# The second MLP layer of the last batch as seven block products (Strassen) on one Trainium2 core

## The chip, the cores and the metric

One core of one Trainium2 chip runs the whole program. The metric is the time of one execution on the device in microseconds (us). A change counts as faster or slower when the 95% interval of the ratio is clear of 2%, as the same when the interval lies within 2%, else as unclear.

In the profiles, PE is TensorE (matmuls), PEld its weight loads, DVE VectorE, ACT ScalarE, POOL GpSimd, SP the engine that issues transfers. L173 and the like are lines of the program; one helper at L173 issues nearly all matmuls, so one tells groups apart by the tiles that they write and read.

## The reference, cut to what matters

```python
# block-sparse attention of 4 batches, 8 heads, 768 positions, 64 per head -> x: (4, 768, 512)
scores = scale * q @ k^T;  scores = where(mask, scores, -1e9);  attn = softmax(scores)
x = (attn @ v) with the heads side by side
# mixer on x
h = (x^T @ U @ V)^T            # U: 768x32, V: 32x768
u = x + h
out = u + relu(u @ w_ch1) @ w_ch2      # w_ch1: 512x2048, w_ch2: 2048x512
```

The change concerns the last product, `relu(...) @ w_ch2`, for the last of the four batches: 768 x 2048 times 2048 x 512.

## The kernel before: the parts that matter

The Python program places every instruction in a fixed order per engine. A small model of time (`clk`) decides, while the program is built, what is put next on TensorE: score units, value products and MLP steps of the batch before are interleaved, so that TensorE always has work. On the chip that order is fixed.

Attention for one head pair has nine units. A unit is: score matmuls into a two-bank PSUM tile (`double`), an exponential on ScalarE into an SBUF tile `est`, then a product with the mask on VectorE, with both inputs in SBUF:

```python
def mask_mul(u, est):
    ...
    nc.vector.tensor_tensor(out=o, in0=o, in1=m, op=ALU.mult)     # 128 x 1024, f16
    return 1.25 if clk["pool"] > clk["dve"] else 0.69             # us, for the model
```

After nine units come the values (`pav`, 72 matmuls), a normalization on VectorE (`rcp`, `xs`), a cast on GpSimd (`xh`), the low-rank product (`pa`), its sum on VectorE (`a`), the second one (`ph`), and the addition `xf` on VectorE. GpSimd also issues the loads of q, k and v:

```python
def unit_sides(i, u):            # called when unit u of head pair i is put in order
    ...
    if u in (3, 5, 7):
        load_cast(i + 2, {3: "q", 5: "k", 7: "v"}[u])             # GpSimd issues two transfers
```

PSUM has eight banks, used as four tiles of two banks each, handed out by `double(name)` and given back by `give_back`. The second layer of the last batch used one bank of such a tile per 128 rows (a row group):

```python
def w2(sc, part, n0, n1):
    if part == 0:
        pair["pch"] = double("pch")                  # tile [128, 2, 512] f32
    pch = pair["pch"][:, 0:1, 0 : n1 - n0]
    for jj in range(4 * part, 4 * part + 4):         # 16 in all
        mm(pch[:, 0, :], tT[jj][:, sc * P : (sc + 1) * P], w2t[:, jj, n0:n1], jj == 0, jj == NJJ - 1)
    if part == 3:
        leave(sc, 1, n0, n1, pch, pair["pch"])       # one VectorE addition, one transfer out
```

The softmax here doesn't subtract the row's maximum and nothing guards it: scores larger than these inputs give would overflow.

## Time and profile before

| | before |
|---|---|
| time, median of 4 runs (lowest, highest) | 278.81 us (277.80, 279.37) |
| span of the profiled execution | 276.6 us |
| first layer of the last batch, 128 matmuls | 232.09 to 252.90 us |
| second layer of the last batch | 252.90 to 273.82 us: 20.92 us |
| last matmul's end to the end of the span | 2.8 us |

The lines behind these numbers are in the prediction below.

One view: the mask products as a group, with busy time, mean ns of one, and idle time before them. In the kernel before:

```profile
L520 DVE TENSOR_TENSOR est<-est,m 128x1024 f16<-128x1024 f16 x108 | 78.3, 740 | 18.2 <-ACT est L499 16.8
```

### The profile page before, as it was taken

Reading aid. Unit: us, or ns where it says so; the run is one execution under the profiler, and the core shown is the slowest. Engines: PE = TensorE matmul, PEld = TensorE weight load, DVE = VectorE, ACT = ScalarE, POOL = GpSimd, SP = SyncE. Lnnn points to the kernel's source line nnn. Section 1 sums busy time; section 2 is a strip of 40 time slices with the busy share of each in tenths; the row PEclk is TensorE's granted clock in tenths of the full one; section 3 lists DMA queues with packets and bytes.
Section 4 is the critical chain, followed back from the end, with each engine's and each line's share of the span. In section 5 each row is a group of like instructions: output and inputs, shape, how many; then the busy total and the mean of one; then the engine's idle time right before and its main releaser. Section 6 shows DMA issues by size and latency. Waiting matters only on the chain.

```text
span 276.6 us, 8037 instructions
## 1 busy us (share of the span) xinstructions
PE 270.9 (98%) x3493; PEld 161.8 (59%) x3493; DVE 175.2 (63%) x286; ACT 177.3 (64%) x198; POOL 103.2 (37%) x137
## 2 busy tenths in 40 slices
PE   8999999999999999999999999999999999999995
PEld 2577775565656564656565565656565654665443
DVE  6877758878797987777756768777777451000112
ACT  3999995877897857694955749584886201664000
POOL 5659639407274835363604536361102020000000
PEclk9999999999999999999999999999999999999999
DMA  6999976999979999996990989995100322000222
GB/s 202 287 297 258 264 172 104 165 185 87 142 47 107 174 125 145 157 105 73 59 112 0 189 88 164 135 100 74 31 2 2 104 79 79 27 1 0 78 77 76
DMA packets 85484, 31.65 MB, mean 114 GB/s; under 512 B 75152, under 2 KB 83048, under 8 KB 85448
## 3 DMA queue, kind: packets, MB, share of 16 engines
q0 software_dynamic: 49824, 10.29, 43.8%
q1 hardware_dynamic: 35268, 20.62, 34.7%
q8 instruction: 27, 0.44, 0.7%
q10 hardware_dynamic: 356, 0.22, 0.3%
q14 instruction: 9, 0.07, 0.1%
HBM read 27.84 MB, written 6.29 MB: 123 GB/s over the span
## 4 chain that ended last, share of the span: by engine, by line
PE 83%; ACT 11%; DVE 2%; DMA 1%; issue 1%; POOL 1%; SPq 0%; DVEq 0%; POOLq 0%; ACTq 0%
PE pch L173 30%; PE pt L173 30%; ACT est L499 11%; PE pav L173 11%; PE psc L173 9%; PE pa L173 2%; DMA qld<-in_q_dram 1%; PE ph L173 1%; POOL xh L599 0%; DVE xh L542 0%; DVE xs L590 0%; PE pmk L173 0%; POOL qst L247 0%; PE pturn L266 0%; PE puT L704 0%
## 5 line engine op out<-in xcount | busy, mean ns | idle before, releaser
L499 ACT ACTIVATE est<-psc 128x1024 f16<-128x1024 f32 x144 | 143.2, 1028 | 45.4 <-PE psc L173 43.7
L173 PE MATMUL pt<-uT,w1t 64*128 64x384 f16 (+1 forms) x896 | 94.4, 324 | 0.0
L173 PE MATMUL pch<-w2t,tT 64*128 64x512 f16 (+3 forms) x688 | 93.6, 372 | 0.1
L520 DVE TENSOR_TENSOR est<-est,m 128x1024 f16<-128x1024 f16 x108 | 78.3, 740 | 18.2 <-ACT est L499 16.8
L173 PEld LDWEIGHTS <-w1t 64*128 64x128 f16 (+1 forms) x896 | 46.0, 95 | 36.1 <-PE pt L173 8.3
L173 PEld LDWEIGHTS <-tT 64*128 64x128 f16 (+1 forms) x688 | 38.2, 95 | 36.9 <-PE pch L173 1.6
L737 ACT ACTIVATE tT<-pt 128x768 f16<-128x768 f32 (+1 forms) x48 | 36.6, 772 | 26.0 <-PE pt L173 26.0
L173 PEld LDWEIGHTS <-est 128*128 128x128 f16 x1152 | 41.5, 97 | 10.9 <-issue 5.0
L173 PE MATMUL pav<-vt,est 128*128 128x65 f16 x1152 | 44.5, 193 | 0.1
L792 DVE TENSOR_TENSOR of<-xf,pch 128x1024 f32<-128x1024 f32 (+3 forms) x16 | 15.2, 950 | 42.7 <-PE pch L173 42.7
L173 PE MATMUL psc<-qT,kT 64*128 64x512 f16 (+1 forms) x288 | 40.6, 323 | 0.3 <-ACT est L499 0.3
L599 POOL CAST xh<-xs 128x768 f16<-128x768 f32 x12 | 10.5, 872 | 79.1 <-DVE xs L590 73.5
L685 POOL CAST uh<-xf 128x768 f16<-128x768 f32 x12 | 14.0, 1163 | 26.1 <-DVE xf L676 14.5
L173 PE MATMUL psc<-qa,ka 128*128 128x512 f16 (+1 forms) x96 | 21.7, 326 | 0.4 <-ACT est L499 0.2
L739 DVE TENSOR_SCALAR tT<-pt 128x768 f16<-128x768 f32 (+1 forms) x20 | 18.3, 917 | 5.9 <-PE pt L173 5.8
L173 PEld LDWEIGHTS <-kT 64*128 64x128 f16 x288 | 14.6, 94 | 12.5 <-issue 0.7
L261 POOL DMA_DIRECT2D vt<-in_v_dram x20 | 16.3, 821 | 3.8 <-DMA w2t<-in_moe_w_ch_dram 3.8
L261 POOL DMA_DIRECT2D qst<-in_q_dram x20 | 16.3, 820 | 0.1
L261 POOL DMA_DIRECT2D kst<-in_k_dram x20 | 16.3, 819 | 0.0
L590 DVE TENSOR_TENSOR xs<-pav,rcp 128x768 f32<-128x768 f32 x12 | 11.5, 958 | 1.2
L676 DVE TENSOR_TENSOR xf<-xs,ph 128x768 f32<-128x768 f32 x12 | 11.4, 950 | 1.2 <-PE ph L173 1.2
L173 PEld LDWEIGHTS <-ka 128*128 128x128 f16 (+1 forms) x108 | 8.7, 97 | 3.9 <-issue 2.0
(70 smaller groups left out, 131.2 us busy)
## 6 DMA issues: line engine op xcount, KB each, us to landing
out_dram<-of SPq DMA_DIRECT2D x9, 512.0 KB, 3.3
vld<-in_v_dram SPq DMA_DIRECT2D x6, 384.0 KB, 8.0
w1t<-in_moe_w_ch_dram POOLq DMA_DIRECT2D x4, 512.0 KB, 9.2
w2t<-in_moe_w_ch_dram POOLq DMA_DIRECT2D x4, 512.0 KB, 11.0
qld<-in_q_dram SPq DMA_DIRECT2D x5, 384.0 KB, 7.2
kld<-in_k_dram SPq DMA_DIRECT2D x5, 384.0 KB, 8.3
qst<-in_q_dram POOLq DMA_DIRECT2D x20, 96.0 KB, 4.1
kst<-in_k_dram POOLq DMA_DIRECT2D x20, 96.0 KB, 4.6
```

What stands on the lines that cost most here:

```text
L173: ins = nc.tensor.matmul(out, lhsT, rhs, start=start, stop=stop, skip_group_check=loose)
L261: keep(nc.gpsimd.dma_start(out=o[:, h], in_=src_of(nm, i)[:, h]))
L499: keep(nc.scalar.activation(out=est, in_=psc, func=AF.Exp, scale=0.125))
L520: keep(nc.vector.tensor_tensor(out=o, in0=o, in1=m, op=ALU.mult))
L590: nc.vector.tensor_tensor(out=xs.rearrange("p (c j) (h d) -> p c (j h) d", c=2, h=2), in0=pv[:, :, :, 0:D], in1=rcp[:, :, :, None].broadca ...
L599: keep(nc.gpsimd.tensor_copy(out=xh, in_=xs))
L676: nc.vector.tensor_tensor(out=u.rearrange("p (c j) n -> p c j n", c=2), in0=xs.rearrange("p (c j) n -> p c j n", c=2), in1=ph[:, :, 0:HS]. ...
L685: keep(nc.gpsimd.tensor_copy(out=uh, in_=u))
L737: keep(nc.scalar.activation(out=o, in_=i, func=AF.Relu))
L739: keep(nc.vector.tensor_scalar_max(out=o, in0=i, scalar1=0.0))
L792: nc.vector.tensor_add(out=of, in0=xfs[b][:, sc : sc + nsc, n0:n1], in1=pch)
```

## The change

The intent: a product of two 2x2 block matrices needs seven block products in place of eight, so TensorE streams an eighth less in that layer. The price is sums of blocks. Five sums of weight blocks go to GpSimd, in ten instructions amid attention; the sums of activation blocks go to VectorE during the first layer, where it is idle; and the outputs are put together by VectorE, in place in `xf`. Cut to its core:

```diff
+    W_SUMS = {"11+22": ..., "12-22": ..., "21-11": ..., "11+12": ..., "21+22": ...}
+    def add_w2(n):                                  # n = 0..9
+        ...                                         # even n: 6 of 8 blocks (1536), odd n: 2 of 8 (512)
+        keep(nc.gpsimd.tensor_tensor(out=o, in0=w2_block(x0, y0, j0, j1),
+                                     in1=w2_block(x1, y1, j0, j1), op=op))
...
+        def add_t(j):                               # activations, VectorE, after two relus
+            for o, i0, i1, op in (
+                (both, lo, hi, ALU.add),                               # 768 elements
+                (diag, lo[:, 0:HS], hi[:, HS:S], ALU.add),             # 384
+                (lo[:, HS:S], lo[:, HS:S], lo[:, 0:HS], ALU.subtract),
+                (hi[:, 0:HS], hi[:, 0:HS], hi[:, HS:S], ALU.subtract),
+            ): keep(nc.vector.tensor_tensor(out=o, in0=i0, in1=i1, op=op))
...
-        for jj in range(NJJ):                       # order of the first layer's blocks
+        for jj in range(NJJ) if rowed else [j + x * NJ for j in range(NJ) for x in range(2)]:
...
-        def w2(sc, part, n0, n1): ...
+        def w2_product(g, n, j0, j1, n0=0, n1=HB):  # g: pair of row groups, n: product
+            if n == 3 and j0 == 0: pair["ab", g] = double("pab")       # both banks in one tile
+            if n == 1 and j0 == 0: pair["c", g] = double("pc")
+            bank, at = {3: (0, 0), 5: (0, HB), 4: (1, 0), 2: (1, HB), 1: (2, 0),
+                        6: (0, 0), 7: (1, 0)}[n]
+            o = c[:, 0, 0:HB] if bank == 2 else ab[:, bank, at : at + HB]
+            for j in range(j0, j1): mm(o, t_sum[n, j][:, g * P : (g + 1) * P], w[:, n0:n1], ...)
+            def run(eng):                           # VectorE, when the model has time for it
+                if n == 5: acc(c11, ab[:, 0, HB:512], ALU.subtract); acc(c12, ab[:, 0, HB:512])
+                           acc(c12, ab[:, 0, 0:HB]); send(c12)
+                if n == 2: ...                      # three or four sums out of ab[:, 1]
+                if n == 1: ...                      # c11 and c22 from c
+                if n == 6: acc(c22, ab[:, 0, 0:HB]); send(c22)
+                if n == 7: acc(c11, ...); send(c11, n0, n1)
...
+        for g in range(3):
+            for n in (3, 5, 4, 2, 1, 6, 7): ...     # the last of all in two pieces of columns
...
     def unit_sides(i, u):
+        if u in (1, 6) and i in range(2 * HP, 3 * HP + 1):
+            add_w2(2 * (i - 2 * HP) + (u == 6))
```

More of the change, by code (lines that the diff above doesn't have):

```diff
@@ L714, in turn_u_pe, with w2_block @@
         run_on("dve", 0.6)
+    NJ, HB = NJJ // 2, HD // 2
+    W_SUMS = {
+        "11+22": (0, 0, 1, 1, ALU.add),
+        "12-22": (0, 1, 1, 1, ALU.subtract),
+        "21-11": (1, 0, 0, 0, ALU.subtract),
+        "11+12": (0, 0, 0, 1, ALU.add),
+        "21+22": (1, 0, 1, 1, ALU.add),
+    }
+    w_sum = {}
+    def w2_block(x, y, j0, j1):
+        return w2t[:, x * NJ + j0 : x * NJ + j1, y * HB : (y + 1) * HB]
+    def add_w2(n):
+        k, part = n // 2, n % 2
+        key = list(W_SUMS)[k]
+        x0, y0, x1, y1, op = W_SUMS[key]
+        if n == 0:
+            for m in range(6):
+                t = ldpool.tile([P, 6, HB], FP16, tag="ld" + "qkv"[m % 3], name="w2s")
+                w_sum["home", m] = t
+        j0, j1 = ((0, 6), (6, NJ))[part]
+        if part == 0:
+            o = w_sum["home", k][:, 0:6, :]
+        elif k < 3:
+            o = w_sum["home", 5][:, 2 * k : 2 * k + 2, :]
+        else:
+            o = qa[0][k - 3].rearrange("p (j n) -> p j n", n=HB)[:, 0:2, :]
+        keep(
+            nc.gpsimd.tensor_tensor(
+                out=o, in0=w2_block(x0, y0, j0, j1), in1=w2_block(x1, y1, j0, j1), op=op
+            )
+        )
+        for j in range(j0, j1):
+            w_sum[key, j] = o[:, j - j0, :]
     def mlp_steps(b):
@@ L741, in run @@
                 give_back(pt, clk[eng] + us)
+                if not rowed:
+                    jj = tiles[0][0]
+                    full.add(jj)
+                    if (jj + NJ) % NJJ in full:
+                        later("dve", 1, lambda e: add_t(jj % NJ), clk[eng] + us)
                 return us
@@ L749, in tile_of @@
             return tT[jj]
+        rowed = b < B - 1
+        full, t_sum, added = set(), {}, set()
+        def add_t(j):
+            lo, hi = tT[j], tT[NJ + j]
+            if j % 2 == 0:
+                t_sum["two"] = new_est().rearrange("p a n -> p (a n)")
+            both = new_est().rearrange("p a n -> p (a n)")[:, 0:S]
+            diag = t_sum["two"][:, (j % 2) * HS : (j % 2 + 1) * HS]
+            for o, i0, i1, op in (
[3 more added lines that the diff above has]
+                (hi[:, 0:HS], hi[:, 0:HS], hi[:, HS:S], ALU.subtract),
+            ):
+                keep(nc.vector.tensor_tensor(out=o, in0=i0, in1=i1, op=op))
+            t_sum[1, j] = diag
+            t_sum[2, j] = both[:, HS:S]
+            t_sum[3, j] = lo[:, 0:HS]
+            t_sum[4, j] = hi[:, HS:S]
+            t_sum[5, j] = both[:, 0:HS]
+            t_sum[6, j] = lo[:, HS:S]
+            t_sum[7, j] = hi[:, 0:HS]
+            added.add(j)
+            return 1.5
@@ new lines, in force, with acc, send @@
+        def force(done):
+            while not done():
+                clk["pe"] += 0.05
+                run_engines(clk["pe"])
+        def w2_product(g, n, j0, j1, n0=0, n1=HB):
+            if n == 3 and j0 == 0:
+                pair["ab", g] = double("pab")
+                pair["done", g] = set()
+            if n == 1 and j0 == 0:
+                pair["c", g] = double("pc")
+            ab, c, done = pair["ab", g], pair.get(("c", g)), pair["done", g]
+            if n in (6, 7) and j0 == 0:
+                force(lambda: {6: "a", 7: "b"}[n] in done)
+            bank, at = {
+                3: (0, 0), 5: (0, HB), 4: (1, 0), 2: (1, HB), 1: (2, 0), 6: (0, 0), 7: (1, 0),
+            }[n]
+            fresh = n in (3, 4, 1)
+            o = c[:, 0, 0:HB] if bank == 2 else ab[:, bank, at : at + HB]
+            if n0:
+                o, fresh = c[:, 1, 0:HB], True
+            else:
+                o = o[:, 0 : n1]
+            o = o[:, 0 : n1 - n0]
+            for j in range(j0, j1):
+                force(lambda: j in added)
+                w = {
+                    1: lambda: w_sum["11+22", j],
+                    2: lambda: w2_block(0, 0, j, j + 1)[:, 0, :],
+                    3: lambda: w_sum["12-22", j],
+                    4: lambda: w_sum["21-11", j],
+                    5: lambda: w2_block(1, 1, j, j + 1)[:, 0, :],
+                    6: lambda: w_sum["11+12", j],
+                    7: lambda: w_sum["21+22", j],
+                }[n]()
+                mm(
+                    o, t_sum[n, j][:, g * P : (g + 1) * P], w[:, n0:n1],
+                    fresh and j == 0, j == NJ - 1, True, us=0.108 * (n1 - n0) / HB,
+                )
+            if j1 < NJ:
+                return
+            last = g == 2
+            xq = xfs[b].rearrange("p t (c n) -> p (t c) n", c=2)
+            c11, c12, c21, c22 = 2 * g, 2 * g + 1, 2 * g + 6, 2 * g + 7
+            def acc(q, i, op=ALU.add, n0=0, n1=HB):
+                o = xq[:, q, n0:n1]
+                keep(nc.vector.tensor_tensor(out=o, in0=o, in1=i, op=op))
+            def send(q, n0=0, n1=HB):
+                t, c = divmod(q, 2)
+                keep(
+                    nc.sync.dma_start(
+                        out=out[b].rearrange("(p t) d -> p t d", t=T)[
+                            :, t, c * HB + n0 : c * HB + n1
+                        ],
+                        in_=xq[:, q, n0:n1],
+                    )
+                )
+            def run(eng):
+                us = 0.34
+                if n == 5:
+                    acc(c11, ab[:, 0, HB:512], ALU.subtract)
+                    acc(c12, ab[:, 0, HB:512])
+                    acc(c12, ab[:, 0, 0:HB])
+                    send(c12)
+                    done.add("a")
+                    us = 1.0
+                if n == 2:
+                    acc(c22, ab[:, 1, HB:512], ALU.subtract)
+                    acc(c21, ab[:, 1, HB:512])
+                    if last:
+                        acc(c11, ab[:, 1, P:HB], n0=P)
+                    acc(c21, ab[:, 1, 0:HB])
+                    send(c21)
+                    done.add("b")
+                    us = 1.2 if last else 1.0
+                if n == 1:
+                    o = xq[:, c11 : c22 + 1 : c22 - c11, :]
+                    i = c[:, 0, None, 0:HB].broadcast_to([P, 2, HB])
+                    keep(nc.vector.tensor_tensor(out=o, in0=o, in1=i, op=ALU.add))
+                    if not last:
+                        give_back(c, clk["dve"] + 0.6)
+                    us = 0.6
+                if n == 6:
+                    acc(c22, ab[:, 0, 0:HB])
+                    send(c22)
+                if n == 7:
+                    i = c[:, 1, 0:HB] if n0 else ab[:, 1, 0:HB]
+                    acc(c11, i[:, 0 : n1 - n0], n0=n0, n1=n1)
+                    send(c11, n0, n1)
+                    if n1 == HB:
+                        give_back(ab, clk["dve"] + 0.34)
+                return us
+            if n in (5, 2, 1, 6, 7):
+                later("dve", 2, run)
@@ L824, in w2_rows @@
                 leave(s0, 2, 0, HD, pair["pch"], pair["pch"])
-        def w2(sc, part, n0, n1):
-            if part == 0:
-                pair["pch"] = double("pch")
-            pch = pair["pch"][:, 0:1, 0 : n1 - n0]
-            for jj in range(4 * part, 4 * part + 4):
-                mm(
-                    pch[:, 0, :],
-                    tT[jj][:, sc * P : (sc + 1) * P],
-                    w2t[:, jj, n0:n1],
-                    jj == 0, jj == NJJ - 1, us=0.217 * (n1 - n0) / HD,
-                )
-            if part == 3:
-                leave(sc, 1, n0, n1, pch, pair["pch"])
-        rowed = b < B - 1
         if b == 0:
@@ L877, in mlp_steps @@
             return steps
-        for sc in range(T):
-            for n0, n1 in [(0, HD)] if sc < T - 1 else [(0, 384), (384, HD)]:
-                for part in range(4):
-                    steps.append(
-                        (
-                            0.87 * (n1 - n0) / HD,
-                            lambda sc=sc, part=part, n0=n0, n1=n1: w2(sc, part, n0, n1),
-                            "" if part else "open",
+        for g in range(3):
+            for n in (3, 5, 4, 2, 1, 6, 7):
+                for n0, n1 in [(0, HB)] if (g, n) != (2, 7) else [(0, P), (P, HB)]:
+                    for j0 in range(0, NJ, 4):
+                        steps.append(
+                            (
+                                0.434 * (n1 - n0) / HB,
+                                lambda g=g, n=n, j0=j0, n0=n0, n1=n1: w2_product(
+                                    g, n, j0, j0 + 4, n0, n1
+                                ),
+                                "open" if n in (3, 1) and j0 == 0 else "",
+                            )
                         )
-                    )
         return steps
```

## The prediction

> **What bounds the kernel now.** I read the page's busy shares first, then the row of forty slices, then the granted clock in stretches of time, and last the timeline of the stretches that the change touches.
>
> ```profile
> PE 270.9 (98%) x3493; PEld 161.8 (59%) x3493; DVE 175.2 (63%) x286; ACT 177.3 (64%) x198; POOL 103.2 (37%) x137
> ...
> PE   8999999999999999999999999999999999999995
> PEld 2577775565656564656565565656565654665443
> DVE  6877758878797987777756768777777451000112
> ```
>
> TensorE is at nine tenths in every slice but the first and the last, and the chain of waits gives it 83% of the span. Busy time alone would not prove a bound, since matmul ends are modelled, so I added up the spacings that the timeline shows: 768 half-height first-layer matmuls at 0.082 us (16 in 1.31), 576 half-height second-layer ones at 0.1085 (8 in 0.87), 108 score units at 0.22, 12 times 2.39 for the values and 0.5 for the small products: 184 us, some 2 us of them before 47.7. The stretch from 47.7 to 232 is 184 us long. So TensorE's order is packed; a delay of it by another engine goes straight into the end time, as does work taken from it. The clock granted is 1.00 in all stretches to 270 us.
>
> The part that changes is the last 44 us:
>
> ```profile
> 232.09 20.97 PE L173 MATMUL pt<-uT,w1t 128*128 128x384 f16 x128
> ...
> 252.90 20.92 PE L173 MATMUL pch<-w2t,tT 128*128 128x512 f16 x112
> ...
> 272.97 0.56 DVE L792 TENSOR_TENSOR of<-xf,pch 128x384 f32<-128x384 f32 x1 [1.91 <-PE pch L173]
> 273.86 0.29 DVE L792 TENSOR_TENSOR of<-xf,pch 128x128 f32<-128x128 f32 x1 [0.34 <-PE pch L173]
> ```
>
> Columns are start, duration, engine, line, operation. Here TensorE is alone: VectorE is idle but for one addition per output row group, GpSimd is wholly idle. The last addition ends at 274.15, the span at 276.6: 2.45 us for the last transfer to land.
>
> **What the Trainium skill says.** (1) "TensorE: Matmul & The Clock Gate", Back-to-back issue gap: N/2.4 + 2.5 ns warm. The trace agrees: the second layer is 96 matmuls' worth of 512 columns, 20.9 us / 96 = 218 ns against 216. For 256 columns that makes 109 ns, and the weight loads should keep up, as 72 loads with matmuls of only 65 columns took 2.45 us here (34 ns a pair). (2) "VectorE: DVE Perf Modes", The perf-mode tier table: a tensor_tensor on 16-bit data in SBUF runs at two elements a cycle, with PSUM at one. The trace agrees: 1024 f16 elements in 0.69 us; 128, 384 and 512 f32 elements from PSUM in 0.29, 0.56 and 0.69 us. (3) "SBUF — State Buffer", Who interferes with whom: a VectorE instruction with two SBUF inputs and a GpSimd instruction that reads SBUF exclude one another for a whole instruction. The trace shows it:
>
> ```profile
> 95.03 1.17 POOL L685 CAST uh<-xf 128x768 f16<-128x768 f32 x1 [1.32 <-issue]
> ```
>
> ```profile
> 95.43 1.31 DVE L520 TENSOR_TENSOR est<-est,m 128x1024 f16<-128x1024 f16 x1
> ```
>
> The cast takes 0.83 us where it meets no mask product; here it takes 1.17, having waited for the mask product in front, and then the next mask product takes 1.31 instead of 0.69. (4) "GPSIMD Engine Reference", 3.1 Elementwise: about 2.6 cycles per element for a two-input operation, 4497 ns for 2048 f32 elements. No such instruction is in the trace, so this one is taken on trust: 2.2 ns an element.
>
> **The change, part by part.**
>
> Removed and added on TensorE, second layer of batch 3: before, 6 row groups x 16 x 512 columns = 49,152 columns; after, 3 pairs of row groups x 7 products x 8 x 256 = 43,008. By 109 ns for 256 columns: 168 x 0.109 = 18.3 us against 20.9, a gain of 2.6 us. Everything ahead of that stage has the same order on TensorE, ScalarE and VectorE in both programs, line by line; only GpSimd has ten instructions more.
>
> Added on VectorE, first layer: four sums per block index, 8 times. From 0.69 us for 1024, with 0.52 ns an element: 768 elements 0.56 us, 384 elements 0.36 us, so 0.56 + 3 x 0.36 = 1.6 us per 2.6 us of TensorE. It fits beside, VectorE and GpSimd being idle there. Only the last sum is exposed: the last relu ends at about 253.97, the sum that product five needs at 254.6, and TensorE arrives there at 254.5. The order 3, 5, 4, 2 hides the rest: 0.2 us lost.
>
> Added on VectorE, second layer: per pair of row groups, 8 sums into the output. 256 elements are 0.42 us (from the three durations above), so 3 x 0.42 twice, 0.69, and 0.42 twice: 4.1 us beside 6.1 us of TensorE. At the end it is tighter: product two's four sums (1.55 us) begin some 2.5 us before TensorE's end, then come product one's (0.69), six's and the two pieces of seven. I get VectorE's last sum 0.9 us after TensorE's end, against 0.35 before. A further 0.1 us for product seven waiting until its bank has been read.
> Tail: -2.6 + 0.2 + 0.55 + 0.1 = about -1.8; the landing time of the last transfer stays 2.45. I say -1.9 us, with product five's wait perhaps smaller.
>
> Added on GpSimd, amid attention (from about 96 to 172 us): five sums of 1536 elements, estimated at 2.2 ns each 3.4 us, and five of 512, 1.2 us: 23 us. GpSimd has room; the point is the lock. Each holds off VectorE's mask products for its length. I placed each by its neighbours in GpSimd's order and looked at what stands next in VectorE's and TensorE's order:
> - First long sum, at 96.2, right after the cast above. Lock from 96.6 to 99.9. The mask product it meets at 96.66 is the last of its head pair (the scores started at 93.74, the exponential at 94.17), for which the values' matmuls wait:
>
> ```profile
> 98.40 2.45 PE L173 MATMUL pav<-vt,est 128*128 128x65 f16 x72
> ```
>
>   They could start at 100.55 at the earliest: 2.1 us lost.
> - Second, at 109.1 to 112.5: two mask products slide from 109.98 and 111.06 to 112.5; the normalization behind them, at 112.37, to 113.7. The cast and matmuls that follow had 0.27 us to spare: about 1.1 us lost.
> - Third, at 129.5 to 132.9, just ahead of this:
>
> ```profile
> 129.77 0.68 DVE L520 TENSOR_TENSOR est<-est,m 128x1024 f16<-128x1024 f16 x1
> 130.44 0.96 DVE L739 TENSOR_SCALAR tT<-pt 128x768 f16<-128x768 f32 x1
> 131.31 0.28 DVE L628 CAST a<-pa 128x128 f16<-128x128 f32 x1
> ...
> 132.11 0.33 PE L173 MATMUL ph<-a,Vd 64*128 64x128 f16 x6
> ```
>
>   The mask product at 129.77 holds up a relu and the cast of `a`; TensorE's ph, with 0.2 us to spare, would start near 135: 2.9 us lost.
> - Fourth and fifth, at 146.8 and 162.6: VectorE has only PSUM reads or nothing there; about 0.
> - The short ones: four fall beside PSUM reads or idle time, one delays a last mask product by 0.3 us.
> Sum: 2.1 + 1.1 + 2.9 + 0.3 = 6.4 us lost, if both the 2.2 ns and the lock hold for this operation. With the tail that gives 278.84 + 6.4 - 1.9 = 283.3 us.
>
> **The rivals.**
> *A: the plain gain.* GpSimd's sums cost nothing that is seen, because they are shorter on f16, or let the mask products in between, or TensorE has more slack than I read. For it: the sums' places look chosen, and the mid stage keeps all other orders. Against it: the cast of 0.83 us already shows the lock. Time: 278.84 - 1.9 = 276.9.
> *B: short sums.* At half the duration (1.7 us), the first costs 0.5, the second nothing, the third 1.3: 1.8 us lost, so gain and loss cancel: 278.7. With two port reads an element at one a cycle, which is what the one-input cast (about 0.83 ns an element, from 768 and 384 elements) would suggest doubled, the sums last 2.7 us and cost 1.4 + 0.4 + 2.1: 3.9 us, so 280.8.
> *C: the full lock, as summed above:* 283.3.
> *D: the tail gives the gain back:* the sums on VectorE become the bound of the second layer. Against it: 4.1 us of work to 6.1. Even if every sum took half as long again, it would just fit; it can cost 1 us at the very end.
> *E: later loads of q, k and v,* queued behind the sums. They were issued some 8 us before the transposes that read them, so 3.4 us vanish.
>
> **Range and chances.** I give A 30%, B in its two forms 30%, and C with its neighbourhood 40%. The middle of these lies near 281, which is where I put it, between the short and the full lock; the range runs from A to a full microsecond past C. To be faster by 2% it would have to save 5.6 us, twice the most that TensorE's removed columns give: 1%. Slower by 2% starts at 284.4, which needs C and another microsecond: 10%. Else within 2%: 89%.
>
> **What would show it.** In the changed kernel's profile: (a) the second layer of the last batch: 168 matmuls in 18.1 to 18.6 us; (b) the first layer as long as before, with the sums beside it; (c) last addition 0.9 us after the last matmul; (d) GpSimd's long sums: 2.7 to 3.5 us, the short ones 1.0 to 1.3; (e) mask products of 3 us and more beside the first three long sums; (f) the start of the last batch's first layer, 232.09 before, moved to 236 to 239. Were (f) at 232 to 233, the lock's cost would be wrong and A right. If long mask products are there but (f) has hardly moved, TensorE had slack that I didn't see. If the stage of (a) were over 20 us, weight loads or product waits would be the error.

## The result and the profile after

| | before | changed |
|---|---|---|
| time, median of 4 runs | 278.81 us | 292.93 us (292.47 to 294.69) |
| span of the profiled execution | 276.6 us | 291.3 us |
| first layer of the last batch begins | 232.09 us | 240.44 us |
| first layer lasts | 20.81 us | 20.81 us |
| second layer | 20.92 us | 26.9 us |
| last matmul's end to the end | 2.8 us | 3.2 us |

The ratio is 1.052, with a 95% interval of 1.047 to 1.058: slower. A ratio is the mean time of one kernel's fast runs over that of the other's in the same rounds, so it is not quite the ratio of the medians. The time lies far outside the predicted range.

The 14.7 us of span fall into three parts: 8.35 us by which the last batch's first layer begins later, 6.0 us by which the second layer is longer, and 0.4 us at the very end. TensorE's own work shrank as planned; two things new to its path cost more.

**The tail.** The timeline of the changed kernel for the last batch, TensorE and VectorE lines (start, duration, engine, line, operation, and in brackets idle time before it and what ended it):

```profile
240.44 20.97 PE L173 MATMUL pt<-uT,w1t 128*128 128x384 f16 x128
...
261.25 1.04 PE L173 MATMUL pab<-w2s,tT 128*128 128x256 f16 x8
262.13 1.13 PE L173 MATMUL pab<-w2t,est 128*128 128x256 f16 x8
...
263.09 1.04 PE L173 MATMUL pab<-w2s,tT 128*128 128x256 f16 x8
...
264.23 1.21 DVE L871 TENSOR_TENSOR xf<-xf,pab 128x256 f32<-128x256 f32 x3 [0.51 <-PE pab L173]
...
265.49 1.03 PE L173 MATMUL pab<-w2t,est 128*128 128x256 f16 x8 [1.36 <-DVE xf L871]
```

These are products 3, 5, 4 and 2 of the first pair of row groups. Product 5 ends at 263.26 and VectorE is free at 263.72, when its last activation sum ends, but it begins the sums of product 5 at 264.23, after product 4, whose bank it doesn't read. Then product 2 begins at 265.49, when those sums have ended, though it writes the bank that they don't read. The two engines take turns. The list of waits of the changed kernel (waiter, whom it waited for, total us, times, longest) has the sum of it:

```profile
DVE xf L871 <- PE pab L173: 12.8, 12, 1.8
...
PE pab L173 <- DVE xf L871: 6.8, 9, 1.4
```

Nine waits of TensorE: 6.8 us. In the timeline, each of the nine is a product that goes to one bank while the sums that it waits for read the other. At each of them the overlap of one matmul's end with the next one's start is lost as well, some 0.16 us, as a matmul of 256 columns lasts 0.27 us in the trace but follows the one before by 0.108: 9 x 0.16 = 1.5 us. With 18.3 us of matmuls that makes 26.6 of the 26.9 us.

**Amid attention.** Long sums of the changed kernel on GpSimd, from its timeline:

```profile
96.19 3.53 POOL L749 TENSOR_TENSOR w2s<-w2t 128x1536 f16<-128x1536 f16 x1
...
111.93 3.10 POOL L749 TENSOR_TENSOR w2s<-w2t 128x1536 f16<-128x1536 f16 x1
...
135.36 3.08 POOL L749 TENSOR_TENSOR w2s<-w2t 128x1536 f16<-128x1536 f16 x1
```

The mask products that VectorE had next, from its timeline in short windows:

```profile
96.69 3.58 DVE L520 TENSOR_TENSOR est<-est,m 128x1024 f16<-128x1024 f16 x1
```

```profile
110.76 4.82 DVE L520 TENSOR_TENSOR est<-est,m 128x1024 f16<-128x1024 f16 x1
```

```profile
135.67 3.32 DVE L520 TENSOR_TENSOR est<-est,m 128x1024 f16<-128x1024 f16 x1
```

Each of them normally lasts 0.69 us. TensorE then waited, as the timeline of its instructions shows:

```profile
115.64 1.28 PE L173 MATMUL pav<-vt,est 128*128 128x65 f16 x26 [2.49 <-DVE est L520]
...
140.43 0.34 PE L173 MATMUL ph<-a,Vd 64*128 64x128 f16 x6 [2.26 <-DVE a L629]
```

And the group of mask products, 740 ns on average before, is now

```profile
L520 DVE TENSOR_TENSOR est<-est,m 128x1024 f16<-128x1024 f16 x108 | 92.3, 878 | 13.2 <-ACT est L499 11.9
```

To see where TensorE fell behind, I compare the start of the low-rank product `pa` of each head pair in both traces (TensorE's order is the same in both up to the last batch's second layer):

| `pa` before, us | 92.15 | 103.39 | 114.90 | 130.24 | 147.03 | 223.46 |
|---|---|---|---|---|---|---|
| changed, later by | 0.04 | 1.68 | 5.90 | 5.89 | 8.34 | 8.35 |

Three steps, one behind each of the first three long sums: 1.6, 4.2 and 2.4 us. The second is larger than the pause of 2.49 us. The table of stretches of the changed kernel shows why (stretch, busy us and instructions of PE, PEld, DVE, ACT, POOL, then the granted clock, DMA share, GB/s):

```profile
113.20:115.60 2.40, 0.00 (x0) 0.00 (x0) 2.40 (x2) 0.00 (x0) 1.82 (x1) 1.00 2.50 105
116.20:119.40 3.20, 3.20 (x30) 1.73 (x29) 2.40 (x4) 0.13 (x1) 0.91 (x2) 0.50 0.60 101
```

The first stretch is the pause. Shortly after it the granted clock was 0.50 for the whole of the second stretch, 3.2 us (the trace's clock records have it from 116.13 for 3.41 us), which is about 1.7 us of work lost: 2.5 + 1.7 = 4.2. The pause itself holds the delay of the short sum at 106.42 too.

### The profile page after: what moved, and what is told of

Same layout as the page of the kernel before. It is cut to its first block, busy times and chain, and to the rows that moved or that the text cites. A ratio compares the mean times of both kernels' runs of the same rounds, so it can differ in the third digit from the quotient of the medians.

```text
span 291.3 us, 8241 instructions
## 1 busy us (share of the span) xinstructions
PE 272.5 (94%) x3557; PEld 169.1 (58%) x3557; DVE 207.5 (71%) x340; ACT 177.2 (61%) x198; POOL 126.3 (43%) x147
## 4 chain that ended last, share of the span: by engine, by line
PE 79%; DVE 14%; ACT 3%; DMA 2%; issue 1%; POOL 1%; SPq 0%; DVEq 0%; POOLq 0%
PE pt L173 27%; PE pch L173 18%; PE psc L173 11%; PE pav L173 11%; DVE est L520 7%; PE pab L173 6%; DVE xf L871 3%; ACT est L499 3%; DMA kld<-in_k_dram 2%; PE pa L173 2%; PE ph L173 1%; PE pturn L266 1%; DVE tT L779 1%; DVE xf L676 1%; POOL xh L599 0%
## 5 line engine op out<-in xcount | busy, mean ns | idle before, releaser
L520 DVE TENSOR_TENSOR est<-est,m 128x1024 f16<-128x1024 f16 x108 | 92.3, 878 | 13.2 <-ACT est L499 11.9
L173 PE MATMUL pch<-w2t,tT 64*128 64x512 f16 x576 | 73.5, 380 | 0.1
L173 PEld LDWEIGHTS <-est 128*128 128x128 f16 x1224 | 48.8, 98 | 16.4 <-issue 6.5
L173 PEld LDWEIGHTS <-tT 64*128 64x128 f16 (+1 forms) x680 | 37.5, 95 | 34.5 <-issue 7.4
L173 PE MATMUL pav<-vt,est 128*128 128x65 f16 x1152 | 45.2, 194 | 2.8 <-DVE est L520 2.7
L749 POOL TENSOR_TENSOR w2s<-w2t 128x1536 f16<-128x1536 f16 (+1 forms) x8 | 20.5, 2565 | 0.1
L871 DVE TENSOR_TENSOR xf<-xf,pab 128x256 f32<-128x256 f32 (+1 forms) x25 | 9.5, 407 | 13.0 <-PE pab L173 12.8
L173 PE MATMUL pab<-w2s,tT 128*128 128x256 f16 (+1 forms) x84 | 11.6, 268 | 5.5 <-DVE xf L871 5.5
L964 DVE TENSOR_TENSOR of<-xf,pch 128x1024 f32<-128x1024 f32 x9 | 10.9, 1215 | 6.5 <-PE pch L173 6.5
```

The lines of the kernel that those rows point to most:

```text
L173: ins = nc.tensor.matmul(out, lhsT, rhs, start=start, stop=stop, skip_group_check=loose)
L520: keep(nc.vector.tensor_tensor(out=o, in0=o, in1=m, op=ALU.mult))
L749: nc.gpsimd.tensor_tensor(out=o, in0=w2_block(x0, y0, j0, j1), in1=w2_block(x1, y1, j0, j1), op=op)
L871: keep(nc.vector.tensor_tensor(out=o, in0=o, in1=i, op=op))
L964: nc.vector.tensor_add(out=of, in0=xfs[b][:, sc : sc + nsc, n0:n1], in1=pch)
```

## The experiments

**Two theories and their rivals.** For the tail: the two banks of `pab` are one tile, and the program's automatic semaphores guard that tile as a whole, so TensorE and VectorE wait for each other without need. The rival: VectorE's output sums are too slow, and the data itself makes TensorE wait. For the middle: GpSimd's sums, which read SBUF, hold VectorE's two-input mask products off (the port lock). The rival: GpSimd is late with the casts and loads that stand behind the sums in its queue.

The first four runs cross the two repairs. All runs gave correct results.

### e1: three banks as three tiles

```diff
-            if n == 3 and j0 == 0: pair["ab", g] = double("pab")
+            if n == 3 and j0 == 0: pair["a", g] = double("pab")
+            if n == 4 and j0 == 0: pair["b", g] = double("pb")
-            o = c[:, 0, 0:HB] if bank == 2 else ab[:, bank, at : at + HB]
+            o = (a, b2, c)[bank][:, 0, at : at + HB]
-   ... ab[:, 0, ...], ab[:, 1, ...] in the sums
+   ... a[:, 0, ...], b2[:, 0, ...]; a is given back after product 6, b2 after 7
```

> Undoes one thing: the three banks of a row-group pair become three PSUM tiles instead of a two-bank tile and a one-bank tile, so that TensorE's writes to one bank no longer carry a semaphore wait on VectorE's reads of the other. GpSimd's sums stay. Theory (shared tile): the 9 waits of TensorE on the output sums (6.8 us) and the half dozen refills shrink to those that the data needs; second layer from 26.8 us to 18.5-20 us, whole 285-286.5 us. Rival (VectorE's output sums are the bound): second layer stays above 24 us, whole 290-293 us.

Measured: 283.97 us (283.34 to 284.51), ratio to the kernel before 1.019 (1.017 to 1.021): unclear. The second layer took 260.75 to 279.37, 18.62 us. In the timeline of this run, the first pair of row groups:

```profile
260.75 1.04 PE L173 MATMUL pab<-w2s,tT 128*128 128x256 f16 x8
261.63 1.13 PE L173 MATMUL pab<-w2t,est 128*128 128x256 f16 x8
...
262.59 1.04 PE L173 MATMUL pb<-w2s,tT 128*128 128x256 f16 x8
...
263.14 1.20 DVE L874 TENSOR_TENSOR xf<-xf,pab 128x256 f32<-128x256 f32 x3
263.46 1.04 PE L173 MATMUL pb<-w2t,est 128*128 128x256 f16 x8
264.34 1.04 PE L173 MATMUL pc<-w2s,est 128*128 128x256 f16 x8
```

The same matmuls and sums, each as long as before, but product 2 (263.46) follows product 4 at the usual distance and runs beside VectorE's sums. The run's list of waits has none of TensorE on them any more. The time came out a microsecond better than I had written. The rival falls: VectorE was not the bound of this stage. That one tile for both banks brings the waits is shown by this run; by what rule the program's semaphores are placed is not.

### e2: the weight sums on VectorE, late

```diff
-            add_w2(2 * (i - 2 * HP) + (u == 6))                  # GpSimd, pairs 8 to 12
+        if i == NPAIR - 1:                                       # after the last pair's xf
+            for n in range(10):
+                later("dve", 4, lambda e, n=n: (add_w2(n, nc.vector), (0.96, 0.42)[n % 2])[1],
+                      clk["pe"] + 1.5)
```

> The ten sums of weight blocks go from GpSimd amid attention to VectorE after its last attention work (between 227 and 236 us of the kernel before), tiles as in the changed kernel. Theory (port lock): the last batch's first layer starts at 232-233 us again instead of 240.4, second layer unchanged at 26-27 us, whole 284-285.5 us. Rival (the stall in mid kernel has another cause): start stays past 236, whole over 288.

Measured: 284.75 us (284.10 to 285.46), ratio 1.022 (1.020 to 1.024): slower. The first layer began at 232.44 us, the second took 26.9 us with the same nine waits (6.8 us). VectorE did a sum of 1536 in 0.95 us, where GpSimd took 3.1 to 3.5, and did all of them in time that was almost free: one addition of an earlier output stood among them, 0.1 us later than before.

### e3: both

The edits of e1 and e2 together.

> Both edits together. If both theories hold and add up: first layer starts at 232-233 us, second layer 18.5-20 us, whole 276.5-278.5 us, a little under the kernel before (278.8). If the gains do not add, over 280.

Measured: 276.46 us (276.09 to 278.34), ratio 0.994 (0.991 to 0.996): the same as the kernel before by the 2% rule, and 0.6% less on the mean. From its timeline:

```profile
231.79 20.98 PE L173 MATMUL pt<-uT,w1t 128*128 128x384 f16 x128
...
252.60 1.04 PE L173 MATMUL pab<-w2s,tT 128*128 128x256 f16 x8
...
270.94 0.28 PE L173 MATMUL pc<-qa,tT 128*128 128x128 f16 x2
271.25 0.29 DVE L880 TENSOR_TENSOR xf<-xf,pc 128x128 f32<-128x128 f32 x1
```

The second layer is 252.60 to 271.22, 18.6 us: 2.3 us less than before. The end gave back 0.6 of them: the span ends 3.4 us after the last matmul, not 2.8. The last three transfers now follow one another within a microsecond, and the last one is issued 0.4 us after its addition has ended; that this is the reason was not tested.

The changed kernel is 292.9; e1 takes off 9.0 and e2 8.2; their sum would give 275.8, and both together give 276.5. So two causes, independent but for 0.7 us, make up the whole loss. (The kernel before had a median of 278.6 in the rounds of e1 to e4, 278.8 in those of the changed kernel.)

### e4: the same GpSimd time without reads

e3, and at the old places memsets on GpSimd into the buffers that VectorE fills later, three in a row (1.4, 1.4 and 0.7 us) for a long sum and one for a short sum:

```diff
+                for w in ((6, 6, 3), (6,))[n % 2]:
+                    keep(nc.gpsimd.memset(w_sum["home", n // 2][:, 0:w, :], 0.0))
```

> Both edits, and at the sums' old places GpSimd gets memsets of about the same length that write SBUF and read nothing (results stay right). Theory (VectorE is locked out of the port by GpSimd's reads): mask products keep 0.7-0.9 us on average and the last batch's first layer starts at 232-233.5 us, within 1 us of the run with both edits. Rival (GpSimd is merely late with its casts and loads): start at 236 us or later, whole 4 us or more above the run with both edits.

Measured: 276.39 us (276.26 to 276.68), ratio 0.992 (0.991 to 0.994). GpSimd was busy 24.5 us with them, more than the 23.2 us of the sums, and its casts and loads stood behind them. Nothing came of it: the first layer began at 231.62, and the mask products of this run were

```profile
L520 DVE TENSOR_TENSOR est<-est,m 128x1024 f16<-128x1024 f16 x108 | 79.0, 747 | 18.0 <-ACT est L499 16.6
```

So the rival falls too. It is not the time that GpSimd took that held VectorE up, but something that the sums do and the memsets don't; they differ in that the sums read SBUF, which fits the rule that the prediction cites.

### e5 to e8: each sum alone

The prediction had a cost for each sum. These runs are e3 with some of the sums left on GpSimd at their old places (`ON_POOL = (0,)`, `(2,)`, `(4,)` and `(1, 3, 5, 7, 9)`), the others late on VectorE. They were run on another chip. Each was run once; I read how much later TensorE's `pa` and `ph` come behind the sum than ahead of it, against the kernel before. The kernel before took 278.21 us in the same round.

> Both edits, but the first long sum alone stays on GpSimd at its old place (the other nine on VectorE). If each sum costs for itself what I worked out: TensorE 2.1 us later behind it (1.65 us in the changed kernel), first layer of the last batch at about 233.5-234 us.

> The second long sum alone on GpSimd. My sum said 1.1 us; in the changed kernel TensorE slid 4.2 us there. If that excess came of the first sum's delay and the short sum before it (VectorE behind when the second sum takes the port): now 0.8-1.5 us and no drop of the granted clock, first layer at 232.6-233.3 us. If the second sum costs that by itself: 3.5-4.5 us, first layer at 235.3-236.3.

> The third long sum alone on GpSimd, ahead of the relu and the cast of a: 2.9 us by my sum, 2.4 us in the changed kernel; first layer at 234.2-234.7 us.

> The five short sums alone on GpSimd: 0.3 us by my sum, first layer at 231.8-232.4 us. If they cost over 1 us, the port is lost for longer than the 1.2-1.5 us that they last.

| on GpSimd | predicted | alone | in the changed kernel |
|---|---|---|---|
| first long sum | 2.1 | 1.6 | 1.6 |
| second long sum | 1.1 | 1.5 | 4.2 |
| third long sum | 2.9 | 2.5 | 2.4 |
| fourth and fifth | 0 | not run | 0.0 |
| five short sums | 0.3 | 0.8 | within the second's 4.2 |
| sum | 6.4 | 6.4 | 8.3 |

The whole times of these four runs were 278.72, 278.16, 279.53 and 277.77 us. The first layers began at 234.15, 233.59, 234.96 and 233.12, each 0.1 to 0.7 us past the range written. In part the ranges were set too early: they count from e3, whose trace is 0.3 us ahead of the kernel before from the start. So e6 is at the upper end of the first reading: the second sum by itself costs 1.5, not 4.2, without a drop of the clock. In e8 the first short sum alone put TensorE back by 0.8 us, where I had 0.3 for all five.

The second long sum shows a detail. In the run with it alone, GpSimd and VectorE, each from its timeline in short windows:

```profile
108.13 0.82 POOL L261 DMA_DIRECT2D vt<-in_v_dram  x1
108.96 3.10 POOL L753 TENSOR_TENSOR w2s<-w2t 128x1536 f16<-128x1536 f16 x1
```

```profile
108.11 4.51 DVE L520 TENSOR_TENSOR est<-est,m 128x1024 f16<-128x1024 f16 x1 [0.19 <-ACT est L499]
```

The mask product began 0.85 us ahead of the sum's recorded start and still lost to it: it ended 0.6 us after the sum. In front of the sum stood the issue of a transfer. My working took the recorded start as the moment at which VectorE is held off. So a third mask product was caught, 0.6 us more, while the sum came out 0.3 us shorter than assumed; that is most of the difference between 1.1 and 1.5. Why VectorE is held off earlier is open: the legend of the profile calls spans on GpSimd rough, so the sum may have been at work before its recorded start.

### e9 and e10: where the rest comes from, and whether length counts

e9 leaves the five long sums on GpSimd and puts the short ones on VectorE; e10 has all of them on GpSimd, but in twenty pieces of 512 elements, at units 0, 2, 4 and 6 of the same head pairs. Both have separate tiles. They were run on another chip.

> Separate tiles, the five long sums on GpSimd, the five short ones on VectorE. Alone, the first three long sums cost 1.6, 1.5 and 2.5 us. If costs add up: first layer at 237-238 us. If the extra 1.9 us of the changed kernel (half clock for 3 us after a pause of 2.5) needs only the long ones: 239-240.5 us and a clock below 1.00 in the stretch after the second sum. If it needs the short sum between the first and the second as well: 237-238 and no drop.

> Separate tiles, all sums on GpSimd as in the changed kernel but in twenty pieces of 512 elements (1.2-1.5 us each, four a head pair) in place of five of 1536 and five of 512. GpSimd's time stays (24-28 us). Theory (one lock per instruction, paid where VectorE's next work is due on TensorE's path): each block is at most 1.5 us, first layer at 233.5-236.5 us. If what counts is the total of locked time and not its length: 239-241 us.

e9 measured 283.82 us (the kernel before in that round: 280.29). TensorE fell back by 1.6, 1.4 and 2.4 us behind the first three long sums, as when each was alone, and then by another 1.7 us behind the third: there the granted clock stood at 0.50 from 139 to 142 us. First layer at 239.16, so neither of the outcomes that I had written is quite it: the extra cost came without the short sums, but with a clock drop behind the third sum, not the second. In the changed kernel and in e1 it was the second. So the extra cost is the clock's, about 1.7 us, paid once behind a pause of 2.3 to 2.5 us. Length alone doesn't decide which pause brings it: the third sum alone (e7) made TensorE pause for 2.27 us at the same place as in e9, also 2.27, and the clock stayed at 1.00.

The clock records of the traces show what does. Within a run the clock changes only on a grid of 3.41 us: the two drops of the changed kernel, at 116.13 and at 290.21 behind the last matmul, are 51.0 such steps apart, those of e1 49.0, those of e9 42.0. Cut along the grid of their own run, the two equal pauses look different (e9, then e7; stretch, busy us and matmuls of PE, granted clock, DMA share, GB/s):

```profile
135.17:138.58 3.41, 1.19 (x18) 1.00 0.69 44
138.58:141.99 3.41, 3.41 (x28) 0.50 0.37 40
```

```profile
130.30:133.71 3.41, 2.25 (x36) 1.00 0.00 0
133.71:137.12 3.41, 2.30 (x32) 1.00 0.91 58
```

In e9 one step holds nearly the whole pause, 2.22 us of idle time, and the next one runs at half clock; in e7 two steps hold 1.16 and 1.11. The changed kernel fits: 2.49 in one step ahead of its drop, 1.85 and 0.41 for its later pause of 2.26. In all twelve traces, from the first clock record on and the ends behind the last matmul included, each step with 2.00 us idle or more was followed by half clock, and none with 1.89 or less. (Idle is counted by the matmul ends of the trace, which are modelled.) Where the grid lies differs from execution to execution: its first record stands at 6.90 us in the changed kernel and at 5.82 in e1, though their orders are the same up to the second layer. And in e1, two executions had a mean clock of 0.993 (284.4 and 284.5 us) and two of 0.999 and 1.000 (283.6 and 283.3). So this part of the loss can be in one execution of a program and not in the next.

e10 measured 279.38 us, first layer at 234.81. GpSimd's sums took 28.0 us in all, and the mask products 882 ns on average, as long as in the changed kernel. But TensorE fell back by 3.3 us only, without a drop of the clock (the changed kernel: 8.3 us, 1.7 of them the clock's). So the sum of the blocked time is not what counts. The pieces differ in length and in place (units 0, 2, 4 and 6 in place of 1 and 6), and no run parts the two; that the length of one block counts, against the slack of what TensorE needs next, is the likelier reading and not shown alone.

## Why the prediction was wrong

- **TensorE's part: right.** 18.3 us of matmuls were predicted; the second layer took 18.6 us where nothing else stood in the way (e1, e3).
- **VectorE's sums in the first layer: right.** The first layer kept its 20.81 us, and only product five's last matmul waited, 0.1 us.
- **The tail, -1.9 us: wrong, and the step that failed.** (The terms written add up to -1.75.) The prediction set "4.1 us of work to 6.1" on VectorE, found that it fits, and gave rival D "1 us at the very end" at most. The durations were right; VectorE's sums fit. What failed is the assumption that they lie beside the matmuls. Both banks were in one tile, and each engine waited for the other's use of the whole tile: +6.0 us in place of -2.6 + 0.2 + 0.1. The only wait on a bank that the prediction had was 0.1 us for product seven. The cause stands in the change itself: `double("pab")` hands out both banks as one tile. The end's +0.55 was right in size by luck: VectorE's last sum ended 0.3 us after the last matmul, as before, and not 0.9; what grew, by 0.4 us (0.6 in e3), is the time from there to the landing of the last transfer, which the prediction had as unchanged.
- **The lock amid attention, 6.4 us: right in that the sums hold the mask products off, undersized.** Each sum alone adds up to 6.4 us. Together they cost 8.35. Nearly all of the rest is the granted clock at one half for 3.4 us behind a pause of 2.5, about 1.7 us, which my sum had no term for. The single terms were off both ways: 2.1 for 1.6, 1.1 for 1.5, 2.9 for 2.5, 0.3 for 0.8. For the first two, the path was another one than the prediction had. Behind the first sum the values were not held back as a whole: 46 of their 72 matmuls ran on time and the last 26 waited 0.26 us, then `pa` waited 0.73 us for VectorE. Behind the second it was the last 26 matmuls of the values that waited (1.33 us in e6), not the normalization behind them.
- **The choice: wrong.** My own sum of terms said 283.3. I gave the rivals with shorter sums or no cost 60% between them, because the sums' places "look chosen", and put the number near 281. GpSimd's durations came out as the full-lock sum had them (3.1 to 3.5 us), so even without the tail the sum of the terms was the better number.
- Of the signs that I named: (a) over 20 us, "weight loads or product waits would be the error", which it was; (b) held; (c) 0.3 us, not 0.9, in e3 too, where TensorE is not held back; (d) held for the long sums (3.1 to 3.5 us), but three of the five short ones took 1.5 us, not 1.0 to 1.3; (e) held; (f) 240.4 us, beyond 239.

## What to carry to other kernels

Ask of every wait in the order of instructions which data it protects: a tile that spans two PSUM banks can carry waits from one bank to the other, and a product that fits beside another engine's work on paper then takes turns with it. Put two-input work on GpSimd where VectorE runs no two-input SBUF work; in short pieces it cost less here (e10), but still 3.3 us. VectorE's own idle time at the end of attention took the same sums at a third of the duration and next to nothing. A saving of 2.6 us on the bound engine is easily less than what its side work costs: with both repairs, 0.6% was left.

## What the Trainium skill lacked or had wrong

- "GPSIMD Engine Reference", 3.1 Elementwise, has a measured two-input rate for f32 alone (2.2 ns an element). On f16 the changed kernel shows 3.08 us for 1536 elements and 1.16 us for 512 at best, which is 1.9 ns an element and 0.2 us fixed.
- "TensorE: Matmul & The Clock Gate", Part 1, says that the clock falls back after at least one idle window of about 3.4 us. Here a window need not be idle throughout: of the steps of 3.41 us in these traces, those with 2.00 us idle or more were followed by a clock of 0.50, those with 1.89 or less were not. A pause of 2.27 us brought the drop in e9, where one step held 2.22 of it, and not in e7, where two shared it. The measurement decides: a pause under 2.5 us can cost another 1.7 us.
- No page says that the program's waits can be those of a PSUM tile as a whole when it spans two banks; with a tile for each bank the second layer went from 26.9 us to 18.6.
